# Lightning attention with a low-rank mixer on one core: the side transfers of the attention stage are asked for at other places and from another queue

## The chip, the cores and the metric

The kernel runs on one core of one Trainium2 chip. The metric is the device time of one execution in microseconds. The profile comes from one further execution; it names the engines PE (matmul), PEld (weight load), DVE (VectorE), ACT (ScalarE), POOL (GpSimd) and SP (SyncE, which here only issues transfers).

## The reference, cut to what matters

The first part is a blocked linear attention with decay, for 4 batches, 8 heads, 768 rows and a head size of 64. The second part takes its output as a 768 x 512 matrix per batch, mixes its rows through a rank-32 product with U and V, and puts the result through a two-layer network with a residual. q, k and v come as float32; U, V and both weight matrices come as float64.

```python
for b in range(nb):                                   # blocks of 64 rows
    intra = np.einsum('bhic,bhjc->bhij', qb, kb) * Dmask[None]
    intra = np.einsum('bhij,bhjd->bhid', intra, vb)
    inter = np.einsum('bhid,bhde->bhie', qb * lam_pow[None], kv_state)
    out[:, :, sl] = intra + inter
    kv_state = lam_block[None, :, None, None] * kv_state + np.einsum('bhsd,bhse->bhde', kb_dec, vb)
...
h = xt @ U @ V                                        # xt: (batch, 512, 768)
u = x + h.transpose(0, 2, 1)
ch = np.maximum(u @ w_ch1, 0.0) @ w_ch2
return (u + ch).astype(np.float32)
```

## The kernel before, in words

**Three stages.** The attention stage goes through 24 steps of 128 rows (six for each of the four batches). The first product (`hidden`, lines 837 and 848) multiplies u by `w_ch1`, and the second (`product`, lines 969 to 973) multiplies the result by `w_ch2`. The order of all instructions of the attention stage and of the head of the first product is written out by hand in the list `pieces` and in `rest`: each engine does its own instructions in that order, and SP issues its transfers in that order too, waiting at each for what its buffer or its source needs.

**One step s of the attention stage**, on PE: transposes of q and k of the next step (`prep`, line 361), the product of the scores with v (`intra`, line 459), the state (`state`, line 431), the product with the old state (`inter`, line 470), the scores of the next step (`scores`, line 408). DVE multiplies the scores by the mask (`masked`, line 417) before `intra` can take them. ACT copies transposes out of PSUM (line 367) and the attention output into `x_nat` (line 476). POOL scales q and k (lines 392 and 381).

**Loads of q, k and v** are 256 KB each. q and v have three buffers, k has four. `next_k` and `prep` ask for the next k and q on SP, `next_v` asks for the next v on ACT's queue when `intra` and `state` of the step are through with the buffer.

**The mixer in the attention stage.** After the sixth step of a batch, `low` (line 486) makes the rank-32 product with U, in four groups of 32 partitions. `low_rows` splits it into a high and a low part: `own` copies the four high parts on ACT (line 529) and makes the four low parts on POOL (line 530), and `other` moves each group's result to the neighbouring group with four transfers on SP (line 540). The first of these happens in step 6, then in steps 12 and 18. `mix` (line 563) takes the tile of V (`v_hl`) as weights and these rows (`p_hl`) as the moving side; both lie in the tile `vp`. `mix(0)` stands in step 7, after `inter(7)`. `mixed` (line 575) adds the result to x, `turn` and `split` prepare u for the first product, and `store` writes u back to memory.

**Work on the side.** U, V and the first two tiles of `w_ch1` come as float64 words (line 146) and are turned into float32 by a chain on DVE and ACT (lines 155 to 227). These chains are lists of steps (fetch, one, mantissa, two, three, four, ...), and a table beside each list says at the end of which attention step each is done (`aside`). What a chain wants on ACT is put into the list `late` and done at the next `late` piece. U is asked for before step 0 (`aside(-1)`), between the loads of q2 and k3; V's two halves are asked for at the end of step 0. V's split writes eight pieces of `v_hl`: four on ACT (line 723), two on DVE and two on POOL (line 727).

Of the kernel before, what the change touches and what calls it, by code (L numbers as in the profile page):

```python
# [8 lines left out]
FP32 = mybir.dt.float32  # L9
# [9 lines left out]
def kernel(  # L19
# [251 lines left out]
    def parts(s):  # L271
        return 2 if s == 0 else 1
# [173 lines left out]

    def next_v(s):
        del raw[s, "v"]
        load_next("v", nc.scalar)

    def intra(s):

# [44 lines left out]
    def low_rows(b):  # L497

        pp = pps.pop(b)
        own = [(slice(g * R, (g + 1) * R), slice(g * P, (g + 1) * P)) for g in range(G)]  # L500
        if b == B - 1:
            h, h2, l, l2 = (p_hl[g * R : (g + 1) * R] for g in range(G))
            for rows, cols in own:
                nc.scalar.copy(h[:, cols], pp[rows])

            def low_part():
                for rows, cols in own:
                    nc.vector.tensor_tensor(
                        out=l[:, cols], in0=pp[rows], in1=h[:, cols].bitcast(FP32),
                        op=ALU.subtract,  # L510
                    )

            def spread():
                nc.scalar.copy(h2, h.bitcast(FP32))

            def spread_low():
                nc.scalar.copy(l2, l.bitcast(FP32))

            pps[b] = [low_part, spread, spread_low]
            return  # L520


        def place(g, of, low):
            return p_hl[g * R : (g + 1) * R, low * 2 * P + (of % 2) * P :][:, 0:P]

        def own():
            for g in range(G):
                rows, at = pp[g * R : (g + 1) * R], place(g, g, 0)
                nc.scalar.copy(at, rows)
                nc.gpsimd.tensor_tensor(  # L530
                    out=place(g, g, 1), in0=rows, in1=at.bitcast(FP32), op=ALU.subtract
                )

        def other():
            for g in range(G):
# [4 lines left out]
                nc.sync.dma_start(  # L540
                    out=at[:, :, g % 2].bitcast(FP32), in_=of[:, :, g % 2].bitcast(FP32)
                )

        pps[b] = [own, other]

    def next_of_low(b):
        pps[b].pop(0)()
# [102 lines left out]
    for s in range(NS):  # L650
# [12 lines left out]
        step += [("next_of_low", b - 1)] * (rows and s > NT)  # L663
        step += [("scale", s + 1)] * more
        step += [("mixed", done)] * (mixes and c != 1)
        step += [("late", s - 1)] * (1 < s < NT - 1 or s > NT)
        step += [("turned", done - 2)] * (done > 1 and c == 1)
        step += [("mixed", done + 1)] * (not more)
# [30 lines left out]
    def v_steps():  # L699

        st = {}

        def dst():
            if "v" not in st:
                st["v"] = wconv.tile([P, C], FP32, tag="wf", name="vf")[0 : 2 * R, 0:SH]
            return st["v"]

        def parts(gs):
            for half in range(2):
                rows, cols = slice(half * R, (half + 1) * R), slice(half * SH, (half + 1) * SH)  # L710
                for g in gs:
                    yield v_hl[g * R : (g + 1) * R, cols], rows

        def five():
            st["t"] = t = wconv.tile([P, C], FP32, tag="wt", name="vt")[0 : 2 * R, 0:SH]
            nc.vector.tensor_scalar(
                t.bitcast(U32), st["v"].bitcast(U32), HI, None, ALU.bitwise_and
            )
            on_scalar(high)

        def high():
            for out, rows in parts((0, 2)):
                nc.scalar.copy(out, st["t"][rows])

        def low(g, engine):
            for out, rows in parts((g,)):
                engine.tensor_tensor(
                    out=out, in0=st["v"][rows], in1=st["t"][rows], op=ALU.subtract
                )

        halves = [moe_V[:, half * SH : (half + 1) * SH] for half in range(2)]
        return weight_steps(dst, halves, SH, 2 * R, in_parts=True) + [
            five, lambda: low(1, nc.vector), lambda: low(3, nc.gpsimd),
        ]


# [336 lines left out]
```

## Time and profile before

| | |
|---|---|
| median of 3 executions | 649.1 us (649.07 to 650.27) |
| the profiled execution: its own time, its span | 649.85 us, 648.1 us |
| PE busy | 639.3 us |
| PE busy in the attention stage, 5.74 to 114.39 us | 105.06 of 108.65 us |
| DVE, ACT, POOL busy in the same stretch | 78.47, 70.19, 74.87 us |
| DMA share, 5.74 to 37.52 us | 1.03 |
| DMA share, 92.83 to 114.39 us | 0.57 |
| transfers from SP's queue (q1), from ACT's (q10) | 124.41 MB, 6.42 MB |
| instruction transfers (q8) | 41, 0.67 MB |

How to read it: the span runs from the first to the last instruction. Matmuls follow each other in a pipeline and their ends are modelled, so that PE can show as busy while it waits a little; the distance between the starts of the scores of two steps is the surer measure of a step. A DMA share of 1 means that all 16 DMA engines had packets all the time, and shares a little over 1 come from packets that overlap.

### The profile page before, as it was taken

To read this page: it belongs to the slowest core of one execution; us is meant where nothing else is said; L and a number is where in the kernel's file an instruction comes from. 1 tells how busy PE (TensorE), PEld (TensorE's weight loads), DVE (VectorE), ACT (ScalarE), POOL (GpSimd) and SP (SyncE) were. 2 spreads that over 40 slices of the span, in tenths; PEclk is the share of its full clock that TensorE was granted. 3 is DMA by queue.
4 is the path that set the end of the run, shared out by engine and by line. 5 is a ranking of instruction groups with operands and counts; after the bars stand their busy time and mean duration, and the time that the engine had idled before them with its cause. 6 is when DMAs were issued, how large, how long until landed. Compare 5 with 4: busy or idle time off the path is not lost.

```text
span 648.1 us, 13405 instructions
## 1 busy us (share of the span) xinstructions
PE 639.3 (99%) x5242; PEld 539.3 (83%) x5242; DVE 434.7 (67%) x709; ACT 268.8 (41%) x500; POOL 116.3 (18%) x104
## 2 busy tenths in 40 slices
PE   9899999999999999999999999999999999999997
PEld 8888989788888888888888888888888888888886
DVE  6656878668997777777796244685575665755854
ACT  3675766435755444444454222332322322322320
POOL 4475968330000000000000000030030300300300
PEclk9999999999999999999999999999999999999999
DMA  9979996354876555655587899864363363543521
GB/s 232 241 182 272 231 242 163 119 191 176 287 258 219 209 207 209 207 209 211 211 292 276 320 332 392 287 220 138 96 227 98 123 204 97 172 152 99 179 82 65
DMA packets 132737, 131.69 MB, mean 203 GB/s; under 512 B 81538, under 2 KB 90754, under 8 KB 132674
## 3 DMA queue, kind: packets, MB, share of 16 engines
q1 hardware_dynamic: 107552, 124.41, 59.1%
q10 hardware_dynamic: 25122, 6.42, 4.4%
q8 instruction: 41, 0.67, 0.4%
q14 instruction: 22, 0.18, 0.1%
HBM read 80.09 MB, written 50.33 MB: 201 GB/s over the span
## 4 chain that ended last, share of the span: by engine, by line
PE 97%; ACT 1%; issue 1%; DMA 1%; DVE 0%; ACTq 0%; DVEq 0%
PE pz L837 27%; PE pd L848 13%; PE pz L971 13%; PE pz L969 13%; PE pd L973 13%; PE px L459 4%; PE pss L408 4%; PE px L470 2%; PE pqk L361 2%; PE pkv L431 1%; PE pm L563 1%; PE pp L486 1%; PE pm L626 1%; DMA kraw<-in_k_dram 1%; PE put L604 1%
## 5 line engine op out<-in xcount | busy, mean ns | idle before, releaser
L837 PE MATMUL pz<-u_hl,w 128*128 128x512 f32 x768 | 185.0, 391 | 0.0
L837 PEld LDWEIGHTS pz<-u_hl,w 128*128 128x128 f32 x768 | 143.7, 188 | 30.2 <-ACT r L844 0.6
L971 PE MATMUL pz<-w_hl,m 128*128 128x512 f32 x384 | 148.7, 389 | 0.0
L969 PE MATMUL pz<-w_hl,m 128*128 128x512 f32 x384 | 148.3, 389 | 0.0
L973 PE MATMUL pd<-w_d,m 128*128 128x512 f32 x384 | 147.4, 389 | 0.0
L952 ACT ACTIVATE m<-rm 128x512 fp32r<-128x512 f32 x96 | 60.6, 632 | 182.3 <-PE pd L973 125.5
L953 DVE SCALAR_TENSOR_TENSOR m<-rm,m 128x512 fp32r<-128x512 f32 x96 | 71.6, 748 | 95.7 <-ACT m L952 95.7
L998 POOL TENSOR_TENSOR o<-o,u 128x512 f32<-128x512 f32 x20 | 29.8, 1523 | 433.1 <-DVE o L994 433.1
L853 DVE SCALAR_TENSOR_TENSOR r<-pd,r 128x512 f32<-128x512 f32 x96 | 61.7, 685 | 60.4 <-ACT r L844 48.2
L848 PE MATMUL pd<-u_d,w 128*128 128x512 f32 x384 | 95.7, 390 | 0.0
L971 PEld LDWEIGHTS pz<-w_hl,m 128*128 128x128 f32 x384 | 72.1, 188 | 15.0
L969 PEld LDWEIGHTS pz<-w_hl,m 128*128 128x128 f32 x384 | 72.1, 188 | 15.0
L973 PEld LDWEIGHTS pd<-w_d,m 128*128 128x128 f32 x384 | 72.1, 188 | 14.7
L848 PEld LDWEIGHTS pd<-u_d,w 128*128 128x128 f32 x384 | 72.0, 188 | 14.9
L844 ACT ACTIVATE r<-pz 128x512 f32<-128x512 f32 x96 | 51.7, 591 | 66.9 <-PE pz L837 66.9
L954 DVE SCALAR_TENSOR_TENSOR m<-m 128x512 fp32r<-128x512 f32 x96 | 74.7, 779 | 3.0
L417 DVE TENSOR_TENSOR sm<-pss,mask 128x512 f32<-128x512 f32 x48 | 30.9, 686 | 18.0 <-PE pss L408 17.8
L215 ACT ACTIVATE w<-wf 128x512 fp32r<-128x512 f32 x32 | 20.3, 633 | 36.5 <-DVE wf L197 28.7
L173 ACT ACTIVATE sc<-sc,ends 128x512 f32<-128x512 uint32 x30 | 21.6, 721 | 22.8 <-DVE sc L166 22.8
L459 PE MATMUL px<-vraw,sm 128*64 128x64 f32 x768 | 29.0, 228 | 1.6 <-issue 1.4
L408 PE MATMUL pss<-qt,kt 64*128 64x128 f32 x384 | 29.0, 290 | 0.6 <-issue 0.5
L459 PEld LDWEIGHTS px<-vraw,sm 128*64 128x64 f32 x768 | 25.9, 140 | 3.4 <-issue 2.5
(91 smaller groups left out, 606.6 us busy)
## 6 DMA issues: line engine op xcount, KB each, us to landing
r_d<-r SPq DMA_DIRECT2D x96, 256.0 KB, 2.5
rm<-r_d SPq DMA_DIRECT2D x96, 256.0 KB, 2.7
words<-in_moe_w_ch_dram SPq DMA_DIRECT2D x30, 512.0 KB, 4.2
w_d<-w SPq DMA_DIRECT2D x16, 768.0 KB, 3.4
w_hl<-w_d SPq DMA_DIRECT2D x16, 512.0 KB, 6.2
u_d<-x_nat SPq DMA_DIRECT2D x24, 256.0 KB, 4.4
u<-u_d SPq DMA_DIRECT2D x24, 256.0 KB, 4.5
qraw<-in_q_dram SPq DMA_DIRECT2D x23, 256.0 KB, 4.8
```

The source lines that it names most:

```text
L408: nc.tensor.matmul(out=pss[:, x, a, :], lhsT=kt[half[x], a, :], rhs=qt[half[x], a, :], start=True, stop=True,)
L459: nc.tensor.matmul(out=px[half[t], x, a, :], lhsT=sm[:, x, a, half[t]], rhs=vr[:, 2 * a + x, :], start=(a == 0), stop=(alone and a == HP - 1),
L837: nc.tensor.matmul(out=like(acc[g][0], g), lhsT=w[:, n, ct, :], rhs=columns(uhl[g][:, n], g, ct), start=(ct == 0 and n == 0), stop=(ct == ...
L844: nc.scalar.mul(rs[g], acc[g][0], 4096.0 + 1.0)
L848: nc.tensor.matmul(out=like(acc[g][1], g), lhsT=w[:, 2, ct, :], rhs=columns(ud[g], g, ct), start=(ct == 0), stop=(ct == CT - 1),)
L853: nc.vector.scalar_tensor_tensor(rs[g], acc[g][1], 4096.0, rs[g], ALU.mult, ALU.add)
L952: nc.scalar.activation(out=m[:, 0], in_=r, func=AF.Relu, scale=NEAR)
L953: nc.vector.scalar_tensor_tensor(m[:, 1], r, 0.0, hi, ALU.max, ALU.subtract)
L954: nc.vector.scalar_tensor_tensor(m[:, 2], hi, E, low, ALU.mult, ALU.subtract)
L969: nc.tensor.matmul(out=pz, lhsT=m[:, 0, cols], rhs=hl[:, 0], start=first, stop=False)
L971: nc.tensor.matmul(out=pz, lhsT=m[:, 1, cols], rhs=hl[:, 1], start=False, stop=end)
L973: nc.tensor.matmul(out=pd, lhsT=m[:, 2, cols], rhs=dd, start=first, stop=end)
```

## The change

- `next_v` asks for v on SP instead of on ACT's queue. The one earlier request for v on ACT's queue (the third v) stays.
- U's words are asked for at the end of step 1 and no longer before step 0; V's two halves at the end of step 2 instead of step 0. U's chain is done in steps 3 and 4 (before: 1 and 2), V's in steps 4 and 5 (before: 3, 4 and 5).
- V's split makes one copy of the high and low parts (two pieces on ACT, two on DVE), and one transfer on SP copies these 64 partitions to the other 64. It stands in the list `late`, so that it is issued in step 6, behind the transfers of `other`.
- For batches 1 and 2, the low parts of the rows' groups 2 and 3 are made on DVE (`own_rest`, before `intra`), no longer on POOL.
- The four quarters of the first tile of `w_ch1` are asked for in steps 6, 7, 9 and 11 (before: 8 to 11), those of the second tile in steps 18 to 21 (before: 14 to 17); its step `one` moves from step 18 to 22.

```diff
     def next_v(s):
         del raw[s, "v"]
-        load_next("v", nc.scalar)
+        load_next("v")
...
+        def low(engine, gs):
+            for g in gs:
+                engine.tensor_tensor(
+                    out=place(g, g, 1), in0=pp[g * R : (g + 1) * R],
+                    in1=place(g, g, 0).bitcast(FP32), op=ALU.subtract,
+                )
+
         def own():
             for g in range(G):
-                rows, at = pp[g * R : (g + 1) * R], place(g, g, 0)
-                nc.scalar.copy(at, rows)
-                nc.gpsimd.tensor_tensor(
-                    out=place(g, g, 1), in0=rows, in1=at.bitcast(FP32), op=ALU.subtract
-                )
+                nc.scalar.copy(place(g, g, 0), pp[g * R : (g + 1) * R])
+                if g < 2:
+                    low(nc.gpsimd, [g])
+            if b == 0:
+                low(nc.gpsimd, [2, 3])
+
+        def own_rest():
+            if b > 0:
+                low(nc.vector, [2, 3])
...
-        pps[b] = [own, other]
+        pps[b] = [own, own_rest, other]
...
         step += [("mixed", done)] * (mixes and c != 1)
+        step += [("next_of_low", b - 1)] * rows
         step += [("late", s - 1)] * (1 < s < NT - 1 or s > NT)
...
         def high():
-            for out, rows in parts((0, 2)):
+            for out, rows in parts(0):
                 nc.scalar.copy(out, st["t"][rows])
 
-        def low(g, engine):
-            for out, rows in parts((g,)):
-                engine.tensor_tensor(
+        def low():
+            for out, rows in parts(1):
+                nc.vector.tensor_tensor(
                     out=out, in0=st["v"][rows], in1=st["t"][rows], op=ALU.subtract
                 )
+            on_scalar(again)
+
+        def again():
+            nc.sync.dma_start(out=v_hl[half[1]].bitcast(FP32), in_=v_hl[half[0]].bitcast(FP32))
...
-        (u_side, (-1, 1, 1, 2, 2)),
-        (v_steps(), (0, 0, 3, 3, 4, 4, 4, 5, 5)),
-        (w1_steps(0, True, True), (8, 9, 10, 11, 12, 14, 15, 16, 17, 17, 20, 21)),
-        (w1_steps(1, True, True), (14, 15, 16, 17, 18, 22, 23, NS, NS, NS, NS, NS)),
+        (u_side, (1, 3, 3, 4, 4)),
+        (v_steps(), (2, 2, 4, 4, 5, 5, 5, 5)),
+        (w1_steps(0, True, True), (6, 7, 9, 11, 12, 14, 15, 16, 17, 17, 20, 21)),
+        (w1_steps(1, True, True), (18, 19, 20, 21, 22, 22, 23, NS, NS, NS, NS, NS)),
...
     for name in "vkvq":
         load_next(name)
-    aside(-1)
     load_next("k")
```

More of the change, by code (lines that the diff above doesn't have):

```diff
@@ L706, in dst, with parts @@
             return st["v"]
[L708 to L712, printed above, removed]
+        def parts(g):
+            for i in range(2):
+                rows, cols = slice(i * R, (i + 1) * R), slice(i * SH, (i + 1) * SH)
+                yield v_hl[g * R : (g + 1) * R, cols], rows
         def five():
@@ L721, in high @@
         def high():
-            for out, rows in parts((0, 2)):
+            for out, rows in parts(0):
                 nc.scalar.copy(out, st["t"][rows])
-        def low(g, engine):
-            for out, rows in parts((g,)):
-                engine.tensor_tensor(
+        def low():
+            for out, rows in parts(1):
+                nc.vector.tensor_tensor(
                     out=out, in0=st["v"][rows], in1=st["t"][rows], op=ALU.subtract
                 )
-        halves = [moe_V[:, half * SH : (half + 1) * SH] for half in range(2)]
+            on_scalar(again)
+        def again():
+            nc.sync.dma_start(out=v_hl[half[1]].bitcast(FP32), in_=v_hl[half[0]].bitcast(FP32))
+        halves = [moe_V[:, i * SH : (i + 1) * SH] for i in range(2)]
         return weight_steps(dst, halves, SH, 2 * R, in_parts=True) + [
-            five, lambda: low(1, nc.vector), lambda: low(3, nc.gpsimd),
+            five, low,
         ]
```

## The prediction

> **What bounds the kernel now.** I read the page first, then the table of busy times by stage and by step, the chain of waits, and last the timeline around the places that the change touches.
>
> ```profile
> PE 639.3 (99%) x5242; PEld 539.3 (83%) x5242; DVE 434.7 (67%) x709; ACT 268.8 (41%) x500; POOL 116.3 (18%) x104
> ...
> q8 instruction: 41, 0.67, 0.4%
> ```
>
> PE is the bound: 8.8 us of the span are idle. A part of the change can gain only by shortening a wait of PE, and it loses wherever it makes PE wait. All of it lies in the attention stage, so the table by step comes next (from the start of one step's scores to the next; window, its length, then PE's busy time):
>
> ```profile
> 11.14:14.93 3.79, 3.79 (x116) 3.59 (x112) 2.58 (x8) 1.66 (x3) 2.11 (x3) 1.00 1.13 254
> ...
> 18.86:23.42 4.56, 4.07 (x120) 3.67 (x113) 3.93 (x6) 2.62 (x7) 2.05 (x2) 1.00 1.17 253
> 23.42:28.29 4.87, 3.97 (x119) 3.63 (x113) 2.64 (x6) 3.52 (x9) 1.35 (x2) 1.00 1.05 238
> ...
> 46.46:50.78 4.32, 4.32 (x128) 4.08 (x125) 2.91 (x5) 3.17 (x8) 3.56 (x4) 1.00 0.94 250
> ```
>
> The same work takes 3.79 us in step 1 and 4.56 and 4.87 in steps 3 and 4. The chain shows what is in between:
>
> ```profile
> 19.80 0.49 issue
> ...
> 24.88 0.90 issue
> ```
>
> "Issue" means that PE waited for nothing that the profile shows: the first gap lies in the middle of 16 equal matmuls, the second in the middle of transposes. There are six such gaps (also at 35.04, 54.26, 63.76 and 91.67: 0.26, 0.18, 0.23 and 0.43 us), 2.5 us idle together. Counted in PE's records, the distances between them are multiples of 256 but for a record or two, and the page has 41 instruction transfers for 2 x 5242 instructions, so 256 in each: PE waits there for its next piece of instructions. By the starts of the matmuls, which the modelled ends don't touch, these gaps cost 0.7, 1.1, 0.4, 0.4, 0.4 and 0.6 us. The third is covered, since ACT's kt copy releases PE at 37.52 in any case; so 3.2 us.
>
> The next view is the timeline around the first use of the rows that the mixer spreads:
>
> ```profile
> 36.08 3.28 SPq L540 DMA_DIRECT2D vp<-vp  x4
> ...
> 37.42 0.38 ACTq L282 DMA_DIRECT2D vraw<-in_v_dram  x1
> ...
> 39.41 0.58 SPq L282 DMA_DIRECT2D kraw<-in_k_dram  x1
> ...
> 41.16 0.69 PE L470 MATMUL px<-kv,qs 64*64 64x64 f32 x32
> 41.78 0.50 PE L563 MATMUL pm<-vp 64*128 64x256 f32 x4
> ```
>
> SP spends 3.28 us on the four transfers of `other`, while ACT's queue takes the load of v in the middle of them. PE reaches `mix(0)` 0.6 us after the start of `inter(7)`, without a wait. The same place in step 12, on DVE:
>
> ```profile
> 63.98 0.69 DVE L575 TENSOR_TENSOR x_nat<-pm,x_nat 128x512 f32<-128x512 f32 x1
> 65.30 0.42 DVE L437 COPY kv<-px 128x256 f32<-128x256 f32 x1 [0.63 <-PE px L431]
> 65.64 0.42 DVE L166 TENSOR_SCALAR sc<-words 128x512 uint32<-128x512 uint32 x1
> 66.40 1.29 DVE L417 TENSOR_TENSOR sm<-pss,mask 128x512 f32<-128x512 f32 x2 [0.34 <-PE pss L408]
> ```
>
> **The change part by part.**
>
> *v on SP and V's second copy, batch 0.* This is the largest term. SP comes to `next_v(6)` behind q10 (issued at 35.61) and waits there until PE has ended `intra(6)`, at 37.4. `other` stands behind it; its sources are ready from 36.1 on (POOL's row starts at 35.49 and lasts 2.15). Issue: v 0.4 (loads of this size in quiet stretches take 0.37 to 0.58), so 37.8; four transfers, the first 0.75 as in the row of 36.08 taken alone, the others 0.59, each 0.09 apart, so 40.7 instead of 39.36. Behind them stands `again`, which also waits for ACT's two copies: `x_nat(6)` can start at 37.5, since v's issue is gone from ACT, and with two copies of 0.51 (line 723) ACT is done at 39.1. So `again` starts at about 40.8. A transfer of `vp` lands 1.8, 2.7 or 3.8 us after its issue (minimum, median, maximum of twelve, 32 KB each). `again` moves 192 KB, so I take the median: 43.5. The second matmul of `mix(0)`, at 42.0, needs these partitions. PE stops for 0.6, 1.5 or 2.6 us; I take 1.5. Everything on PE waits behind it; SP's k10, first quarter of `w_ch1` and q11 come some 2 us later, which three buffers (12 us) cover. Without that cover it would be the 2 us once.
>
> *`own_rest` in step 12.* The two DVE instructions stand ahead of the kv copy. ACT gives group 2 at 65.2 and group 3 at 65.5. The same form (line 508) takes 1.19 us for four, 0.3 each: they end at 65.84, the kv copy at 66.26, `one` of the first tile (0.42) at 66.68, and the scores' mask starts at 66.70 instead of 66.40. `intra(13)` waits for just this: 0.3 us. An upper bound comes from line 220, a subtraction of two SBUF operands like these: it took 1.36 us at 101.74 with POOL at work and 0.69 at 117.62 without. Twice 0.6 gives 0.9. I take 0.4. [...] In step 18 the same two end before the mask is due (`one` is gone from there): nothing.
>
> *v ahead of `other` in steps 12 and 18.* SP's four end at 68.5 instead of 68.1 and at 96.2 instead of 95.9. In step 13 PE itself is 0.4 late by then: nothing more. In step 19 the last one lands at 97.2 now and is needed at 97.4: 0.1 (nothing to 0.6, if the issue is held up as the 1.28 us at 93.29).
>
> *`one` of the second tile, step 22.* It and `mantissa` stand on DVE between 110.45 and the mask at 111.81: 0.84 us if both take 0.42, 1.9 at the slower durations of these lines (0.62 and 1.24). So nothing to 0.5; 0.1.
>
> *U's chain out of step 1.* Line 184 (0.36 us, to 16.37) holds up the mask of step 2 by 0.2 us and `intra(2)` by 0.13: −0.15. In step 3 U's 2.1 us (0.63, 1.11, 0.36 in the rows) take the place of V's 2.05 (1.16, 0.34, 0.55). In step 4 U's rest and V's start come behind the mask and end by 32.8 to 34.4; the next mask starts at 33.31 and `intra(6)` takes it at 36.27: hidden. `low` needs U at 33.19; it is ready by 32.4. U's words land in 5.2 us, by about 21, and are used at 22.4; V's by 25, used at 32.
>
> *ACT.* v's 0.38 us per step end before `inter` gives ACT its next work (50.23 to 50.60; `x_nat` starts at 50.88): nothing. Step 6 has a 0.15 us wait for kt; two copies less ahead of it: −0.1. POOL loses 2 us of V and twice 1.0 us; PE waits for none of that.
>
> *PE's instruction transfers.* All six gaps lie at high DMA shares. In step 17 the second tile's words (issued 86.66, landed 92.2) lie over the transfer before the gap at 91.67 and move away; in step 10 the same. The early ones see U and V leave one part of a full stretch for another. Between all gone (−3.2) and each of the early ones as long as the longest (+0.6) I take −0.3, since two of the smaller ones lose their neighbour.
>
> Sum: 1.5 + 0.4 + 0.1 + 0.1 − 0.15 − 0.1 − 0.3 = +1.55 us. The profiled execution took 649.85 (span 648.1), 0.75 over the median of 649.1; it would take 651.4, and the median becomes 650.7 (+0.24%).
>
> **The rivals.** About 0.2% (1.3 us) is what a measurement can tell here.
>
> *The instruction waits go (faster).* Place: the gaps in steps 3, 4, 10, 12 and 18; price: up to −3.2 us instead of −0.3. For it: both queues are busy around each of them, and v leaves the second queue. Against: the bytes stay, and SP's queue gets them. The rest of the sum is +1.85, so it decides for faster from 3.15 us on, or from 2.25 if `again` lands at its fastest (0.6). All gone with that: 1.55 + 0.3 − 3.2 − 0.9 = −2.25, so 646.9; I put this case at 647.5. [...]
>
> *The transfers are hidden anyway (no change).* If v's issue and the four behind it run closer together and `again` lands in 1.8 us or less, or PE comes later to `mix(0)`, the 1.5 shrinks to 0 to 0.6. For it: the transfers of step 18 land 1.84 us after the last issue. Against: `other` alone would end at 40.7 and land at 42.5. The time: 649.1 to 649.8; with half of the instruction waits gone as well, 649.
>
> *DVE and POOL stand in each other's way (slower still).* Step 12 at 0.9, steps 18 and 22 at 0.6 and 0.5, `again` at 2.6: +4.0 with the rest, 653.1. The mask waits at each of these places are there already.
>
> **How the numbers follow.** The forecast and the slower rival hold 0.42 and 0.06: slower 0.48. Hidden 0.33. Faster 0.19. The likeliest case alone is 650.4 to 651.7 (`again` from 1.2 to 2.5). The range leaves out half of the faster case and the upper part of the slower one: 648.0 to 652.4.
>
> **What would show it.** In the changed kernel's timeline the L563 matmuls of step 7 start with a gap of 0.6 to 2.6 us behind L470, with SP's v, four `vp` and one more `vp` in a row before it; without that gap the main step is wrong. The mask of step 13 starts 0.3 us or more after PE's last scores. `issue` in PE's waits up to 115 us, 3.3 us now, says whether the instruction waits moved: at 2 us or less the faster rival is right. A wait of PE for u_w in step 5, or for qraw, kraw or vraw, would be a step that I have not seen.

## The result and the profile after

The changed kernel takes 659.7 us in the median (657.3 to 661.6) where the kernel before, on the same chip, takes 649.7 us (649.1 to 650.6). The ratio is 1.0154, with a 95% interval of 1.0125 to 1.0184. The forecast was 650.7 us, in a range of 648.0 to 652.4: the sign was right; the size was 10 us where 1.55 had been forecast. The profiled execution of the changed kernel took 661.6 us, with a span of 659.8 us and a mean granted clock of 0.989 where before it was 1.000 (1 is PE's full clock).

The page of the changed kernel, its line of busy times and two of its queues (packets, MB, share of 16 engines):

```profile
PE 643.8 (98%) x5242; PEld 543.5 (82%) x5242; DVE 436.0 (66%) x713; ACT 268.2 (41%) x498; POOL 113.4 (17%) x98
...
q1 hardware_dynamic: 129472, 130.12, 61.6%
q10 hardware_dynamic: 3282, 0.92, 0.6%
```

SP's queue (q1) now carries nearly everything. PE has as many matmuls as before and is idle for 16.0 us of the profiled execution instead of 8.8; it is also busy for 4.5 us more with the same work. Both lie in the attention stage: the first product starts at 126.15 us instead of 114.39, 11.76 us later, and from there to the end it is 533.7 us in both kernels.

The table of busy times by step of the changed kernel (window, its length, PE, PEld, DVE, ACT and POOL busy, the granted clock, DMA share, GB/s). The windows are steps 3, 4, 7, 8, 13 and 19, each from the start of its scores to the next:

```profile
18.90:22.69 3.79, 3.79 (x118) 3.59 (x112) 2.58 (x5) 2.62 (x7) 2.19 (x2) 1.00 0.86 196
22.69:27.18 4.49, 3.97 (x120) 3.63 (x113) 2.27 (x6) 3.43 (x9) 1.28 (x1) 1.00 0.68 160
37.00:46.19 9.19, 4.77 (x121) 4.30 (x118) 2.15 (x7) 4.26 (x10) 4.57 (x4) 0.93 0.74 169
46.19:52.97 6.78, 6.78 (x127) 6.49 (x126) 3.69 (x6) 1.67 (x3) 1.75 (x2) 0.59 0.93 233
70.65:78.99 8.34, 5.92 (x129) 5.57 (x126) 5.57 (x11) 4.74 (x10) 5.96 (x7) 0.80 0.75 179
101.07:108.67 7.60, 5.69 (x129) 5.23 (x126) 5.00 (x10) 3.92 (x9) 5.96 (x7) 0.85 0.63 160
```

The reader is to see two things. Steps 3 and 4 became shorter (4.55 and 4.87 us before). Steps 7, 8, 13 and 19 became much longer: they were 4.60, 4.37, 4.88 and 4.71 us. And in step 8 PE is busy all the time and still needs 6.78 us: its granted clock is 0.59. From one step to the next, the sum is:

| steps | before, us | after, us | difference |
|---|---|---|---|
| 2, 3, 4, 10, 12, 18 and small ones that became shorter | | | −3.1 |
| 7 and 8 | 8.97 | 15.97 | +7.0 |
| 13 | 4.88 | 8.34 | +3.5 |
| 19 and 20 | 9.15 | 12.36 | +3.2 |
| 6, the start before step 0, and the end behind step 23 | | | +1.2 |

PE's waits in the changed kernel (what it waited for, us in total, times, the longest):

```profile
PE pm L574 <- DMA vp<-vp: 4.1, 2, 2.2
PE px L459 <- ACT u_hl L651: 2.8, 2, 2.4
PE px L459 <- ACT x_nat L476: 1.8, 1, 1.8
PE pqk L361 <- issue: 1.1, 1, 1.1
```

Waits on `issue` fell from 3.3 to 1.1 us: the instruction gaps of steps 3, 4, 10, 12 and 18 are gone, and one is left, of 1.07 us, in step 6. In their place stand four waits that were not there, two for `vp` in step 7 and one each ahead of `intra` in steps 13 and 19 (line 574 is the `mix` that was line 563). PE also waits 0.52 us for `kraw` in step 4, a kind of wait that the forecast had named as a step not seen.

The timeline of step 6 and 7 of the changed kernel, SP and PE (start, duration, what; in brackets the idle time before it and what ended it):

```profile
36.12 0.97 SPq L282 DMA_DIRECT2D qraw<-in_q_dram  x1
37.18 2.24 SPq L282 DMA_DIRECT2D vraw<-in_v_dram  x1
39.51 3.23 SPq L551 DMA_DIRECT2D vp<-vp  x4
42.84 0.54 SPq L744 DMA_DIRECT2D vp<-vp  x1
...
40.69 0.69 PE L470 MATMUL px<-kv,qs 64*64 64x64 f32 x32
43.56 0.35 PE L574 MATMUL pm<-vp 64*128 64x256 f32 x1 [2.18 <-DMA vp<-vp]
45.81 0.76 PE L574 MATMUL pm<-vp 64*128 64x256 f32 x3 [1.89 <-DMA vp<-vp]
```

The row of SP is the one that the forecast described: v, the four of `other`, `again`. But v's issue takes 2.24 us where I had put 0.4, the four start at 39.51 instead of 37.8, `again` at 42.84 instead of 40.8, and PE waits twice, 2.18 us for `other` and 1.89 us for `again`.

Step 12 of the changed kernel, on DVE and POOL, and PE behind it:

```profile
71.25 1.82 DVE L528 TENSOR_TENSOR vp<-p_f,vp 32x128 fp32r<-32x128 f32 x2 [0.61 <-POOL vp L528]
73.10 0.42 DVE L437 COPY kv<-px 128x256 f32<-128x256 f32 x1
73.56 0.71 DVE L166 TENSOR_SCALAR sc<-words 128x512 uint32<-128x512 uint32 x1
74.19 1.27 DVE L417 TENSOR_TENSOR sm<-pss,mask 128x512 f32<-128x512 f32 x2
...
71.65 1.27 POOL L392 TENSOR_TENSOR qs<-qt,powq 128x512 f32<-128x512 f32 x1
...
74.97 1.58 PE L459 MATMUL px<-vraw,sm 128*64 128x64 f32 x32 [2.42 <-ACT u_hl L651]
```

The two subtractions of `own_rest` take 1.82 us together: the first 0.47, the second, started at 71.75, 1.32 us. The second ends at 73.07, 0.15 us after POOL's `qs`, which had started 0.1 us ahead of it. The kv copy, `one` and the mask stand behind it. Step 18 shows the same without `one` (0.52 us for the first, 1.33 for the second, PE 1.79 us idle until 104.77).

What is added by the clock: behind these waits the records show a granted clock of 0.50, from 44.94 to 51.77, from 75.66 to 79.07 and from 106.38 to 109.79 us, 13.65 us in all. Steps 7, 8, 13, 19 and 20 are 13.7 us longer, and PE's waits in them are 8.3 us. I put the other 5.4 us down to the half clock; as a remainder this is an estimate. PE works for all but 0.87 us of those 13.65, so half a clock could cost 6.4 us at most, as an estimate. With it, 8.3 + 5.4 + 1.2 − 3.1 = 11.8 us; since the 5.4 is a remainder, the sum had to close.

### The profile page after: what moved, and what is told of

Same layout as the page of the kernel before. It is cut to its first block, busy times and chain, and to the rows that moved or that the text cites. A ratio compares the mean times of both kernels' runs of the same rounds, so it can differ in the third digit from the quotient of the medians.

```text
span 659.8 us, 13403 instructions
## 1 busy us (share of the span) xinstructions
PE 643.8 (98%) x5242; PEld 543.5 (82%) x5242; DVE 436.0 (66%) x713; ACT 268.2 (41%) x498; POOL 113.4 (17%) x98
## 4 chain that ended last, share of the span: by engine, by line
PE 94%; DMA 2%; DVE 1%; ACT 1%; issue 1%; SPq 0%; ACTq 0%; DVEq 0%; POOL 0%; POOLq 0%
PE pz L851 27%; PE pd L862 13%; PE pz L985 13%; PE pz L983 13%; PE pd L987 13%; PE px L459 4%; PE pss L408 3%; PE px L470 2%; PE pqk L361 2%; DMA kraw<-in_k_dram 2%; PE pkv L431 2%; PE pm L574 1%; PE pp L486 1%; PE put L615 1%; DVE vp L528 1%
## 5 line engine op out<-in xcount | busy, mean ns | idle before, releaser
L392 POOL TENSOR_TENSOR qs<-qt,powq 128x512 f32<-128x512 f32 x20 | 25.5, 1276 | 28.3 <-ACT qt L367 26.5
```

## Experiments

The ratios compare medians with those of the kernel before, run beside it on the same chip; in brackets stands the 95% interval. Steps and waits are of the one profiled execution. The kernels vary by 1.5 to 8 us from one execution to the next, so a step's length tells less than the ratio.

### Parts of the change undone: a1 to a4

My first theory after the result was that the position of v's load, ahead of the four `vp` transfers, makes step 7, and `own_rest` steps 13 and 19. a1 gives the low parts back to POOL; a2 puts v's load behind `other` in steps 6, 12 and 18; a3 does both; a4 gives the low parts back and v's loads to ACT's queue.

```diff
 a1, a3 and a4
-            if b == 0:
-                low(nc.gpsimd, [2, 3])
+            low(nc.gpsimd, [2, 3])
...
 a2 and a3
+        step += [("next_v", s)] * rows
...
 a4
-        load_next("v")
+        load_next("v", nc.scalar)
```

> The changed kernel, but all four low parts of the rows are made on POOL again (own_rest does nothing). Theory: in steps 12 and 18 the second DVE instruction of own_rest stands 1.3 us behind POOL's qs, the mask and x_nat come late, PE idles 2.4 and 1.8 us and its clock then runs at half speed for 3.4 us each time. Then steps 13 and 19 (scores to scores), 8.34 and 7.60 us in the changed kernel, fall to 4.9 and 4.7 and the time by about 6.4 us, to 653 us; step 7 keeps its 9.2 us. Rival: these two steps are long since v's load stands ahead of the four vp transfers on SP; then they stay at 8.3 and 7.6 and the time at 659 to 660.

Measured: 1.0131 (1.0076 to 1.0187). Step 13 fell from 8.34 to 5.53 us, but step 7 stayed at 9.32, and in step 19 (7.23) PE now waits 1.87 us for `vp`.

> The changed kernel, but in steps 6, 12 and 18 v's load is asked for on SP behind the four vp transfers and V's second copy, not ahead of them. Theory: in step 7 PE waits for these transfers since v's load and SP's full queue stand ahead of them. Then they are issued from about 37 us on and not from 39.5, the wait in step 7 falls from 4.1 us to 0.5 to 1.5, the half-speed stretch behind it (44.9 to 51.8) goes, steps 7 and 8 together fall from 16.0 to 9.5 to 10.5 us and the time by about 6, to 654 us; steps 13 and 19 keep 8.3 and 7.6. Rival: V's second copy alone makes the wait, since it needs two ACT copies and 2.9 us to land; then the wait stays at 3 us or more and the time at 657 or above.

Measured: 1.0150 (1.0121 to 1.0178). Step 7 is 9.73 us. The four `vp` transfers are still issued from 38.39 on, and the first issue alone takes 2.29 us, without v's load before it. So the position of v's load is not enough as a cause: SP is held up already by the loads ahead of it.

> Both of the two before in one: low parts on POOL, v's load behind the vp transfers in steps 6, 12 and 18. Theory: the losses add up, 6.4 and 6 us, and what is left are the gains in steps 3, 4, 10, 12 and 18 (2.7 us by the changed kernel's step lengths) less a wait of about 1 us in step 7: 647.5 to 648.5 us, ratio 0.996 to 0.998 to the kernel before. Rival: the gains were an accident of that execution or come from own_rest's shorter POOL work; then 650 us, ratio 1.000 to 1.002.

Measured: 1.0148 (1.0118 to 1.0178). The wait moves: the last quarter of the words of `w_ch1`'s first tile, issued at 66.83, lands late, DVE stands idle for 3.1 us at `one` ahead of the mask, and step 13 takes 10.34 us.

> The changed kernel with all of v's loads on ACT's queue again and the low parts on POOL; U, V and the weight words stay at their new places, and so does V's second copy. Two theories of the gaps between PE's pieces of instructions (2.5 us before, 1.8 us in the changed kernel but at one other place): if they went because all loads come from one queue now, they are back here, steps 3, 4, 10, 12 and 18 have 4.5, 4.9, 4.7, 5.8 and 5.9 us and the time is 650.5 to 651.5; if they went because U's, V's and the weight words stand elsewhere, those steps keep 3.8, 4.5, 4.3, 5.3 and 5.3 us and the time is 647.5 to 648.5. The four vp transfers are issued from 36 us on in both, and V's second copy lands at 42 to 43, so a wait of 0.5 to 1 us in step 7.

Measured: 1.0006 (0.9984 to 1.0028). PE has no wait over 0.7 us any more but the one at the start, and the clock is 1.00. With v on ACT's queue the gaps of `issue` are mostly back too, 2.8 us. So with v's loads and the low parts as before the loss is gone; U's, V's and the weight tiles' new places and V's second copy by one transfer, which a4 keeps, are worth nothing together that these runs could tell.

What differs is seen in the table by stretches of 5 us. The kernel before, then the changed one, then a4 (last two numbers: DMA share, GB/s):

```profile
10.00:15.00 5.00, 5.00 (x144) 4.73 (x140) 2.92 (x9) 1.66 (x3) 3.32 (x4) 1.00 1.15 260
15.00:20.00 5.00, 4.80 (x125) 4.38 (x124) 4.21 (x7) 4.42 (x13) 3.16 (x3) 1.00 1.25 278
20.00:25.00 5.00, 4.59 (x125) 4.25 (x126) 4.12 (x8) 3.06 (x10) 1.28 (x1) 1.00 1.09 246
```

```profile
10.00:15.00 5.00, 5.00 (x146) 4.80 (x142) 2.48 (x7) 1.79 (x4) 3.27 (x4) 1.00 1.04 234
15.00:20.00 5.00, 5.00 (x145) 4.73 (x138) 1.62 (x3) 3.59 (x10) 3.32 (x4) 1.00 0.95 214
20.00:25.00 5.00, 4.48 (x130) 4.08 (x126) 4.24 (x8) 3.21 (x10) 1.27 (x1) 1.00 0.77 174
```

```profile
10.00:15.00 5.00, 4.79 (x136) 4.36 (x134) 2.19 (x7) 1.91 (x4) 3.62 (x4) 1.00 1.14 258
15.00:20.00 5.00, 4.35 (x123) 3.96 (x121) 1.62 (x3) 3.83 (x12) 2.84 (x3) 1.00 1.25 281
20.00:25.00 5.00, 5.00 (x142) 4.73 (x144) 3.79 (x8) 2.84 (x9) 1.27 (x1) 1.00 1.04 247
```

From 10 to 25 us, two queues move 261 and 262 GB/s in the mean, the one queue 207. By 35 us, 27,468 packets of 256 bytes have started instead of 30,411, and SP is still issuing late loads where the `vp` transfers come: each of its last four loads ahead of v took 0.86 to 1.74 us to issue. The rates differ by a fifth. SP spends 13.9 of these 15 us issuing in the changed kernel, so the rows do not tell whether the time to issue or the queue behind it is the limit.

### One part alone: b1 and b2

b1 is the kernel before with v's next loads on SP; b2 is the kernel before with `own_rest`.

```diff
 b1
-        load_next("v", nc.scalar)
+        load_next("v")
...
 b2
         def own():
             for g in range(G):
+                nc.scalar.copy(place(g, g, 0), pp[g * R : (g + 1) * R])
+                if g < 2:
+                    low(nc.gpsimd, [g])
...
+        def own_rest():
+            if b > 0:
+                low(nc.vector, [2, 3])
```

> The kernel before with one line of the change alone: v's next loads are issued by SyncE, so that all loads of 256-B rows go through one queue. Theory (one queue moves those rows too slowly, and SP's queue is still full when the four transfers of `other` are due): the rate between 15 and 25 us falls from 246-278 to 175-215 GB/s, the `vp` transfers of step 7 are issued from about 39.5 on and land at 42.5 or later, TensorE stands still 1.5 to 2.5 us in L574 of that step, and its granted clock is 0.5 for some 3.4 us behind it; the gaps of `issue` in steps 2 to 12 shrink by 2.5 to 3 us as in the changed kernel; steps 13 and 19 stay at 4.9 and 4.7 us. Together 652 to 657 us. Rival (the second copy of V by one transfer and the low parts on VectorE are needed for the loss): the gaps go and nothing takes their place, 646 to 648 us.

Measured: 1.0113 (1.0080 to 1.0147), 658.5 us, a little over the expected band. 228, 201 and 242 GB/s between 10 and 25 us: the rate fell, though less than forecast. The chief waits of PE in b1:

```profile
PE pm L563 <- DMA vp<-vp: 4.1, 4, 2.2
PE px L459 <- ACT kt L367: 2.4, 1, 2.4
```

Step 7 is 7.09 us, with 2.22 us of stillness as the theory said, but without half a clock behind it. Step 19 took 9.65 us, against the expectation: SP's issue of the second weight tile's words was held up, they landed at 97.60, and `one` stood on DVE ahead of the mask until then (2.52 us). So one line of the change is enough for most of the loss, though in step 19 it comes by another way.

> The kernel before with one part of the change alone: in the second and third block VectorE subtracts two of the four low parts, in GpSimd's stead. Theory (VectorE's second subtraction waits for GpSimd's, and what stands behind it on VectorE comes too late for TensorE): the second subtraction takes 1.3 us in steps 12 and 18 where the first takes 0.5, TensorE waits 1.8 to 2.4 us ahead of L459 in steps 13 and 19, these two grow from 4.9 and 4.7 to 6.5 to 8.3 us, the later part of it at a granted clock of 0.5: 653 to 656 us. Rival (as predicted: only some 0.4 us in step 13, none in step 19, because in this kernel the loads are not late and VectorE is ahead of TensorE): 649.5 to 650.5 us.

Measured: 1.0075 (1.0050 to 1.0099), 655.6 us. DVE in step 12 of b2:

```profile
64.31 1.81 DVE L528 TENSOR_TENSOR vp<-p_f,vp 32x128 fp32r<-32x128 f32 x2 [0.62 <-POOL vp L528]
66.15 0.42 DVE L437 COPY kv<-px 128x256 f32<-128x256 f32 x1
66.61 0.72 DVE L166 TENSOR_SCALAR sc<-words 128x512 uint32<-128x512 uint32 x1
```

The second subtraction lasts 1.31 us again. PE waits 1.11 us in step 13 and 2.40 in step 19; step 19 is 8.29 us, step 13 5.61 (under the expected 6.5). Steps 17 and 18 of this execution are 2.9 us longer as well, by a gap of `issue` of 1.68 us at 87.67 and the half clock behind it; nothing here ties that gap to `own_rest`, so not all of b2's loss is shown to be `own_rest`'s. The second subtractions last as long in the other kernels too: 1.32 and 1.33 us in the changed kernel, 1.31 and 1.32 in b2, 1.32 and 1.33 in c1 below. In the six kernels with `own_rest` on DVE all 24 subtractions, the first ones too, end 0.15 us after a POOL instruction that began before them; no run here has one without POOL beside it, so what one takes alone was not shown.

### Is it one queue, or v, or the order? c1, d1, d4, c2

c1 is the changed kernel with q's loads on ACT's queue. d1 is the kernel before with v on SP and q on ACT's queue. d4 is c1 with the low parts on POOL. c2 leaves all loads on SP and puts `other` and `again` on ACT's queue, with the low parts on POOL.

```diff
 c1, d1 and d4
-        load_next("q")
+        load_next("q", nc.scalar)
...
 c2
-                nc.sync.dma_start(
+                nc.scalar.dma_start(
                     out=at[:, :, g % 2].bitcast(FP32), in_=of[:, :, g % 2].bitcast(FP32)
```

> The changed kernel with q's loads of the steps on ScalarE's queue; v's stay on SyncE's, the low parts on VectorE. Theory (what costs is that one queue carries all loads of 256-B rows, whichever load it is): the rate between 15 and 25 us comes back to 245-280 GB/s, the `vp` transfers of step 7 land by 41.5 us, step 7 falls from 9.2 to 5.5-6.5 us and step 8 from 6.8 to 4.5-5.5 us, while steps 13 and 19 stay at 6.5 to 8.3 us for VectorE's sake: 653 to 657 us. Rival (it is v itself that must not stand in SyncE's queue): steps 7 and 8 stay at 9.2 and 6.8 us, 658 to 661 us.

Measured: 1.0090 (1.0060 to 1.0120), 657.0 us. The rate is back (285, 215, 277 GB/s; mean 259), the four `vp` transfers land by 41.8 us, and steps 13 and 19 stay long (8.33, 6.41). But step 7 is 7.25 us: `again`, issued at 39.06, landed at 43.17, and PE waited 2.38 us, until 43.26 (the profile calls this wait `issue`). So two queues give back some 3 to 4 us of the loss.

> The kernel before with v's loads on SyncE's queue and q's on ScalarE's in their stead: as many bytes on each queue as before, V's second copy and all low parts as before. Theory (one queue for all loads costs the rate; which load it is does not matter, but what moving v did to TensorE's gaps of `issue` may stay): 245 to 280 GB/s between 10 and 25 us, the `vp` transfers land before 40.5 us, no stillness over 1.3 us, steps 13 and 19 at 4.9 and 4.7 us; the gaps of steps 0 to 6 shrink by about the 1.3 us by which step 7 began earlier with q on ScalarE's queue in the changed kernel (36.24 against 37.52 us): 647.5 to 649.5 us, below the kernel before. Rival (gaps only move about): within 0.2% of the kernel before, 649 to 651.5 us.

Measured: 1.0129 (1.0099 to 1.0158), 659.2 us. My theory fell here. The rate is that of the kernel before (278, 204, 281), V's copy and the low parts are as before, and still PE waits 2.98, 2.32 and 2.24 us for `vp` in steps 7, 13 and 19. SP and PE in d1, step 6 and 7:

```profile
37.66 0.37 SPq L282 DMA_DIRECT2D vraw<-in_v_dram  x1
38.12 3.00 SPq L540 DMA_DIRECT2D vp<-vp  x4
...
45.66 0.79 PE L563 MATMUL pm<-vp 64*128 64x256 f32 x3 [2.98 <-DMA vp<-vp]
```

SP waits for v's buffer until PE is through with it, issues the load at 37.66, and `other` starts 2.0 us later than in the kernel before (36.08). v's load lands at 41.12 and the first two `vp` right behind it, at 41.28 and 41.45. So order seems to count after all, even at the full rate; e1 below tests it.

> The changed kernel with q's loads on ScalarE's queue and all low parts on GpSimd: what then is left of the change is v's load on SyncE's queue, V's second copy by one transfer, and the places of the words. Theory (the low parts on VectorE cost 5 us of what is left with q on ScalarE's queue, the second copy about 2.4 and the half clock behind it): steps 13 and 19 come back to 4.9 and 4.7 us, step 7 stays at 7.2 us for the second copy: 651 to 653 us. Rival (VectorE's part does not matter once loads are in time): 656 to 657 us as without it.

Measured: 1.0172 (1.0148 to 1.0197), 662.4 us: slower than c1. Steps 7, 13 and 19 are 7.72, 7.75 and 7.67 us, all by waits for `vp` (2.85, 2.63 and 2.33 us). With `own_rest` away the mask is in time, and PE comes to `mix` before the transfers do. The two losses in a step do not add; the longer one covers the other.

> The changed kernel with all loads on SyncE's queue, but the transfers of `other` and V's second copy on ScalarE's, which is otherwise empty of loads here, and the low parts all on GpSimd. Theory (the loads on one queue are late by about three tiles, which the buffers bear; the harm comes from the four small transfers behind them in the same queue): the `vp` transfers land within 2.5 us of their source, TensorE does not stand still over 1.2 us, its clock stays at 1.0, and the gaps of `issue` stay away: 646 to 649 us, below the kernel before. Rival (late loads alone are enough, TensorE waits for q's, k's or v's words instead): step 7 or 8 and those after it are still 1 us and more longer each, 653 to 660 us.

Measured: 1.0135 (1.0100 to 1.0169), 660.2 us. ACT's own work then stands behind the issues: V's two copies on ACT start at 39.44, the copy of qt at 41.08, POOL's `qs` and `ks` come after it, and PE waits 2.61, 2.17 and 2.08 us in `state` in steps 7, 13 and 19. This way out is none.

### The order, and two queues: e1, e2

e1 is d1 with v's load behind `other` in steps 6, 12 and 18. e2 is the changed kernel with all three: q on ACT's queue, v behind, low parts on POOL.

```diff
 e1, against the kernel before (e2: the same and a1's, against the changed one)
-        load_next("q")
+        load_next("q", nc.scalar)
...
-        load_next("v", nc.scalar)
+        load_next("v")
...
+        step += [("next_v", s)] * rows
```

> The kernel before with v's loads on SyncE's queue and q's on ScalarE's, as in the kernel that swaps the two alone, and in steps 6, 12 and 18 v's load behind the four `vp` transfers instead of ahead of them. Theory (a `vp` transfer lands right behind the load issued ahead of it in its queue, and v's load can be issued only when TensorE has used its buffer, 2 us after q's was issued in the kernel before): the first `vp` transfer of step 7 is issued by 36.5 us and all four land by 41 us, TensorE waits less than 0.5 us for them in steps 7, 13 and 19, and these steps come back from 8.0, 7.3 and 7.8 us to 4.6, 4.9 and 4.7 us: 648 to 651 us. Rival (it is not the order, but anything of v's on SyncE's queue, or q's loads on ScalarE's, whose issue there is late): steps 7, 13 and 19 stay at 7 us and above, 657 to 660 us.

Measured: 1.0078 (1.0048 to 1.0109), 656.4 us; the profiled execution took 662.1 us, the longest of six. `mix` in e1, in step 7 and in step 13:

```profile
41.21 0.51 PE L563 MATMUL pm<-vp 64*128 64x256 f32 x4
...
73.73 0.76 PE L563 MATMUL pm<-vp 64*128 64x256 f32 x3 [2.77 <-DMA vp<-vp]
```

Step 7 is 4.60 us as in the kernel before: the first `vp` was issued at 35.51 and all four landed by 40.24. But in steps 13 and 19 PE waited 2.77 and 4.00 us. There the first two `vp` land in 2.2 to 2.7 us, and the fourth takes 4.75 and 5.75 us: q's load, 256 KB, was issued on ACT's queue 0.67 and 1.07 us ahead of it. So the theory is right for step 7 and incomplete: a small transfer can be late with no load just ahead of it in its own queue, and here one stood ahead of it in the other.

> The changed kernel with all three of the suspected causes taken away together: q's loads on ScalarE's queue (two queues carry the loads), v's load behind the four `vp` transfers in steps 6, 12 and 18, all low parts on GpSimd; V's second copy by one transfer stays, behind v's load in step 6. Theory (each of the three is enough to keep the loss, as the kernels that left one or two of them showed at 657 to 662 us): steps 13 and 19 at 4.9 and 4.7 us, step 7 between 4.6 and 7.3 us, for the second copy of V alone: 648 to 653 us. Rival (the loss has a further cause): 656 us or more, with TensorE waiting for `vp` in steps 13 and 19 too.

Measured: 1.0097 (1.0061 to 1.0132), 657.9 us (655.2 in the profiled execution). Step 7 is 7.33 us for `again` alone (2.46 us), steps 13 and 19 are 6.14 and 5.69, with 1.18 and 0.71 us of waiting for `vp`: there too the last `vp` is issued 0.69 and 0.35 us behind q's load on ACT's queue. But it lands in 3.08 and 3.01 us, where e1's, 0.67 us behind such a load, took 4.75; so a load ahead on the other queue does not fix the delay. The median lies in the rival's band, so the three causes were not all.

### The three steps as before, the rest changed: f1, f2

f1 has v on SP except in steps 6, 12 and 18. f2 has in addition q on ACT's queue except in these three steps. Both stand against the kernel before.

```diff
 f1 and f2
+        load_next("v", nc.scalar if s >= NT and s % NT == 0 else nc.sync)
...
 f2
+        load_next("q", nc.sync if s > NT and s % NT == 1 else nc.scalar)
```

> The kernel before with v's loads on SyncE's queue in all steps but 6, 12 and 18, where they stay on ScalarE's as before; nothing else is changed. Theory (what counts in those three steps is which load is issued ahead of the four `vp` transfers, and v's is the late one; the loads that one queue carries more slowly elsewhere are borne by the buffers): TensorE waits less than 0.6 us for `vp` in steps 7, 13 and 19, and the gaps of `issue` of steps 2 to 12 stay smaller than before: 646.5 to 650 us. Rival (the single queue, fuller and slower in the steps ahead, is enough by itself): the `vp` transfers of step 6 are issued from 38 us on and TensorE waits 1.5 us and more in step 7: 653 to 659 us.

Measured: 1.0097 (1.0071 to 1.0124), 657.0 us. Step 7 is nearly whole (5.34, with 0.54 us of waiting). Step 13 (7.22) has 2.21 us of waiting for `vp`, whose first issue took 2.03 us, and in step 19 (8.33) DVE waits 2.58 us for the words, as in b1. So one queue elsewhere is enough for a loss by itself. The rival's time came, but not at its place: in step 6 the first `vp` is issued at 36.03, not from 38 us on, and the loss lies in steps 13 and 19.

> As the kernel that swaps v's and q's loads between the two queues, but in steps 6, 12 and 18 v's load is on ScalarE's queue and q's on SyncE's, as before: two queues carry the loads everywhere, and around the `vp` transfers nothing differs from the kernel before. Theory (loads issued just ahead of the `vp` transfers on either queue make them late, up to 5.8 us for the last one; nothing else does): the last `vp` transfer lands within 3.8 us of its issue in all three steps, TensorE waits less than 0.6 us for them: 647.5 to 651 us. Rival (which queue has which load in the other steps matters as well): TensorE waits for `vp` 1 us and more in at least two of the steps 7, 13 and 19: 654 us and more.

Measured: 1.0058 (1.0035 to 1.0082), 655.0 us (658.6 in the profiled execution). Steps 7 and 13 are 4.79 and 5.60 us (waits of 0.0 and 0.64); in step 19 PE waits 2.76 us: q's load of the next `prep` was issued at 99.06 on ACT's queue, the fourth `vp` at 99.72, and that one took 4.87 us. I had not seen that this q load would come in between. In this kernel too the late transfer is the one with a load just ahead. It is not all of f2's loss: its gaps of `issue` come to 4.0 us, with 1.0 us each in steps 10 and 17, where the kernel before has 3.3.

### The half clock: c3. The second copy: d3

c3 is the changed kernel with 18 matmuls of a zeroed tile ahead of `mix(0)`; d3 makes V's second copy by engines, as before.

```diff
 c3
+            if s == 0:
+                keep_busy(18, "pqk")
...
 d3
-            on_scalar(again)
...
-            five, low,
+            five, lambda: low(1, nc.vector), lambda: low(3, nc.gpsimd),
```

> The changed kernel with 18 matmuls more, of a zeroed tile, whose result nothing reads, ahead of the mixing of the first row in step 7, where TensorE stood still for 2.18 and 1.89 us; at some 0.21 us each they fill 3.8 us of that stretch. Theory (the stillness is paid a second time in the clock: TensorE runs at half speed for some 3.4 us behind it): the granted clock stays at 1.0 from 41 to 52 us, step 7 stays at 9.2 us within 0.4 (it is the transfers that it waits for), and step 8 falls from 6.8 to 4.4 us; steps 13 and 19, left as they are, keep their 7.6 to 8.3 us: 656 to 658 us, 2.0 to 3.4 less than the changed kernel. Rival (the half clock has another cause than the stillness, the load on the chip or the transfers): it stays at 0.5 there and step 8 at 6.8 us; with the fillers' own time 660 us or more.

Measured: 1.0185 (1.0153 to 1.0217). The granted clock between 45 and 52 us, in the changed kernel and then in c3:

```profile
45.00:52.00 7.00, 6.19 (x89) 6.11 (x91) 3.27 (x5) 1.67 (x3) 1.26 (x1) 0.52 1.00 254
```

```profile
45.00:52.00 7.00, 7.00 (x148) 6.42 (x148) 3.67 (x6) 1.74 (x4) 1.59 (x2) 1.00 0.90 225
```

With PE kept busy the clock stays at 1.00, and step 8 falls from 6.78 to 4.43 us, 2.35 us less: the stillness makes the half clock. Step 7 is 9.84 us, 0.65 longer, since there the transfers came later still (`again` landed at 47.06, and the second matmul of `mix(0)` starts at 47.16), and as a whole the kernel is not faster: its profiled execution took 660.9 us, against 661.6. The forecast of 656 to 658 us failed; the mechanism is shown, the gain is not.

> The changed kernel with V's second copy made as before, by ScalarE's and GpSimd's own instructions, in place of the one transfer; all else as changed. Theory (two of SyncE's transfers hold TensorE in step 7, the four of `other` and behind them the second copy, which costs 1.89 us and the half clock): the second wait of L574's line goes, step 7 falls from 9.2 to 7.0-7.5 us, step 8 from 6.8 to 4.5 us, steps 13 and 19 stay at 7.6 to 8.3 us: 655 to 657 us. Rival (only the four of `other` count, the second copy would be there soon enough if they were): no less than 659 us.

Measured: 1.0147 (1.0118 to 1.0176). The second wait of step 7 went, but the first grew to 2.59 us, POOL's share of V's copy held up `state` by 0.77 us, and the half clock came all the same, for 3.4 us instead of 6.8: step 7 is 8.58 us, and steps 7 and 8 together are 14.1 instead of 16.0. The rival's time came (660.1 us): while SP is late with the four of `other`, doing without `again` does not show in the median.

None of these kernels is faster than the kernel before.

## Why the prediction was wrong

- **v on SP and V's second copy (+1.5).** The place, the order of the six issues and the wait of PE in step 7 were right; the gap behind L470 that was to show it is there. Wrong was the price: it is 2.18 + 1.89 = 4.07 us, outside its bounds of 0.6 to 2.6. The step that failed is "v 0.4 (loads of this size in quiet stretches take 0.37 to 0.58)". The stretch was not quiet, because the change itself had put all loads on one queue, which made 207 GB/s where two made 261: v's issue took 2.24 us, and all behind it came late: `again` landed 2.88 us after its issue, near the 2.7 that I took, but was issued 2.0 us later than I had it. With two queues (a4, c1) `other` starts at 35.0 and 36.2 us instead of 39.5. The same step took "three buffers (12 us) cover" for SP's lateness elsewhere. The loads are mostly covered (0.7 us of waiting for `kraw` in the changed kernel, up to 2.2 in a3), and a1, a3, b1 and f1 show that the small transfers and the words behind them are not.
- **The half clock (no term).** A wait was priced once, by its length. The runs show that waits of 1.8 us and more can be paid again: c3 shows 2.35 us of it in step 8, and 5.4 us in all is what the waits leave over.
- **`own_rest` (+0.4, and nothing in step 18).** Mis-sized, and for step 18 wrong. The waits are 2.42 and 1.79 us. I priced the instruction by a free row (0.3 us) and, as a bound, by twice that, since line 220 took 1.36 us beside POOL and 0.69 without. Both were too low: the second subtraction took 1.32 and 1.33 us and ended 0.15 us after POOL's `qs`, which had begun before it. That the first lasts 0.5 and not 0.3 us, and that `one` took 0.71, not 0.42, adds to it. In step 18 I held that the two end before the mask is due; they end at 103.50, the kv copy behind them at 103.94, and the mask starts at 103.98. b2 puts the price of this part alone at up to 4.9 us (0.75%), its gap in step 17 included; in the changed kernel it also hides the late `vp` transfers of steps 12 and 18 (d4).
- **v ahead of `other` in steps 12 and 18 (+0.1).** Too small, though covered in the changed kernel: d4 and d1 show waits of 2.2 to 2.6 us for each step when the mask is in time, q's load on the other queue having its part in them. I took 0.4 us of issue for it, and overlooked that SP waits there until PE frees v's buffer, and that the `vp` transfers then land behind v's 256 KB.
- **PE's instruction transfers (−0.3).** Too small. The faster rival's sign came, with `issue` at 1.1 us: the gaps of its five steps went, which makes them 2.7 us shorter, near its −3.2, while the gap of step 6 grew. The rest outweighed it. That it comes of v's leaving ACT's queue, as that rival said, is not shown: a4 has 2.8 us of gaps with v back on ACT's queue, but d3 and f1, with v on SP (f1 but for three steps), have 2.1 and 2.5. (d1's step 3, 4.93 us, is long by a wait of 0.92 us for ACT's copy of kt and not by such a gap.)
- **U's chain (−0.15), `one` in step 22 (+0.1), ACT (−0.1).** Step 2 is 0.14 us shorter, as said; step 22 is unchanged at 4.3; step 6 is 0.59 longer for a gap of `issue` at 35.00, which covers what ACT may have gained.
- **The slower rival** had the right side and three of its four places (steps 12 and 18 and `again`), and at +4.0 two fifths of the difference of 10.1 us in the medians. My sum was right in its side alone: it had 2.1 us of losses where 8.3 us of waits and some 5.4 us of half clock came, and 0.55 us of gains where steps became 3.1 us shorter.

## What to carry to other kernels

Before a load is moved to another queue, ask what stands behind it there: here the price was that of the small, urgent transfers (4.07 us of waiting for `vp` in step 7) and not of the load, and it came with a fuller queue (207 GB/s on one where two moved 261), which the trace of before did not show. A wait of the matmul engine should be priced with the clock that may fall behind it (0.50 for 3.4 us behind a wait of 1.79 us here), and a VectorE subtraction like those of `own_rest` beside GpSimd with the rest of GpSimd's instruction (1.3 us each for the second ones, where a free row had been put at 0.3). Where several late things end in the same step, undoing one shows the next one: undo them together, and one alone on the kernel before.

## What was not expected of the hardware

- **The clock.** It fell to 0.50 behind waits of 1.79, 2.42 and 2.18 + 1.89 us, for 3.4, 3.4 and 6.8 us; behind waits of 2.22 us (b1, step 7) and 2.46 us (e2, step 7) it stayed at 1.00. The kernel before, whose longest wait inside the stage is 0.9 us, has 1.00 throughout. What it goes with can be read from the times. The three half clocks of the changed kernel start 30.72 us apart, 9 times 3.413, and in all 15 kernels with several half clocks, that at the end of the execution included, the starts lie on such a grid of 3.413 us. If the 18 traces are cut along it, the half clock goes with PE's stillness inside one piece. In the changed kernel's attention stage the pieces with 3.06, 2.42 and 1.91 us of it are the ones with half a clock behind them. In all 18 traces, all 22 pieces at full clock with 1.91 us or more of it are followed by half a clock, none with 1.67 or less is, and from 1.68 to 1.79 us four are and two (a2 and c3, step 19) are not. b1's wait falls into pieces of 1.09 and 1.13 us, e2's into 1.33 and 1.13.
- **One queue and two.** For loads in packets of 256 bytes, the mean from 10 to 25 us is 261 GB/s in the kernel before, and 262, 259, 254, 257 and 261 in a4, c1, d1, e1 and e2, which use two queues. It is 207 in the changed kernel and 224, 209 and 212 in b1, c3 and d3, which use one. Over all kernels it is 245 (b2) to 262 with two queues and 196 (a3) to 224 with one; f1, which uses the second one for three loads of v, has 234. Why one queue is slower, these runs do not show.
- **Small transfers behind large ones.** In most of these kernels a `vp` transfer of 32 KB issued right behind a 256 KB load lands 0.15 to 0.2 us behind that load, in its own queue (v 41.12 and `vp` 41.28 in d1) as in the other one (q 38.88 on ACT's queue, `vp` 39.05 in e1), and up to 5.75 us after its issue (e1, step 19) where 1.8 is the shortest. Why the fourth one of e1 came later still, these runs do not show.
- **What stays open.** What makes the gaps of `issue` come and go is not settled. They come to 3.3 us in the kernel before, 2.8 in a4 and 3.4 in b2, with v's loads on ACT's queue; with v on SP to 1.0 to 2.5 us in most kernels, but to 3.6 and 4.0 in e1 and f2, where ACT's queue has q's loads. (Waits of 2.38, 2.61 and 3.41 us in c1, c2 and a3 that the profile calls `issue` are left out, since they end with a transfer or another engine's work.)
